# Four subtractions of half blocks placed behind two transform blocks of the last chunk

## The chip, the cores and the metric

The kernel runs on one core of a Trainium2 chip. Its time is the device time of the program in microseconds (us), as the median of several runs. A profile is one execution taken by the hardware profiler; the engines are named as in the profile: PE is TensorE (matmuls; PEld its weight loads), DVE is VectorE, ACT is ScalarE, POOL is GpSimd, SP is SyncE, which here only issues transfers.

## The reference

Two sublayers work on the same normalised input and are added to it. All of it is float32, with S = 2048 tokens, D = 640 and F = 1728.

```python
xn = _layernorm(x, axis=-1)
# A: real part of a Fourier transform over the hidden and then over the sequence dimension
a = einsum("bsd,ed->bse", xn, dft_hid_re)
b = einsum("bsd,ed->bse", xn, dft_hid_im)
A = einsum("ts,bse->bte", dft_seq_re, a) - einsum("ts,bse->bte", dft_seq_im, b)
# B: gated feed-forward
gate = einsum("bsd,df->bsf", xn, W_gate)
up   = einsum("bsd,df->bsf", xn, W_up)
B = einsum("bsf,fd->bsd", (gate * (gate > 0)) * up, W_down)
return x + A + B
```

## The kernel before

The kernel has three stages. The *sequence stage* (up to about 408 us) multiplies the normalised tokens with the two sequence matrices first and leaves the products in DRAM. The *gate stage* makes the gate and up products. The *last stage* multiplies both with the hidden matrices and W_down and adds x.

**Products.** Each float32 product is done as three matmuls: an operand is split into a high part (a rounded copy, ScalarE, L131) and a low part (the operand minus its high part, VectorE, L132), and high x high, high x low and low x high are added in PSUM (`mm3`, L137 to L139). The products are taken over 2 by 2 blocks with seven block products instead of eight, so that sums and differences of blocks are operands: they have the names B11, B12, B21, B22 (blocks) and T1 to T4 (differences).

**The sequence stage** goes through four chunks of 512 output columns (c = 0 to 3). In each chunk the units T1, T2 and B22, T3, T4 follow each other, each over four blocks g = 0 to 3; T2 and B22 alternate (T20 B220 T21 B221 T22 T23 B222 B223). A unit of `stream` loads a block of the transform matrix (L716, tile raw or tk, SP's queue), makes the difference on VectorE (L712), the high part on ScalarE and the low part on VectorE into one of three places of a ring (tile cb), and multiplies it with the resident tokens (xs_early, xs_late) or sums of them (gw). `lows` is the list of the low parts in the order in which they were written, so `lows[-1]` is the latest one.

`drive(4, 2)` writes the steps of the units out: a unit's loads four units ahead of its matmuls, its preparation two ahead. After the preparation of a unit, functions that were registered for it with `at(c, name, g, ...)` are called (`hooks`). `defer(1, f)` calls f one unit later.

**Work for the gate stage** is done beside it with these hooks. `token_sets` normalises transposed tokens in a work area, makes their blocks and differences (L411 to L427), splits them and stores both halves to DRAM (L449, GpSimd's queue). `cross_sets(1, work_pair)` rearranges the fifth part of the hidden dimension: `load` (L464, four loads on GpSimd's queue, 64 partitions each) brings the halves into two places of the work area; `subs` are four subtractions of 128x512 on VectorE (L471): t1 = b12 - b11, t2 = b22 - t1, t3 = b22 - b12, t4 = b21 - t2; `keep` stores seven half blocks to the DRAM tile crossed (L475 and L476, six stores on GpSimd's queue). The load is registered at T1 block 0 of the last chunk.

The work area is the tile `late["work"]` in the pool r1, which has a single buffer. In the last chunk the next tile of r1 takes that buffer: `load_halves` (L789, SP's queue) loads the sets T2, T1 and T3 for the gate stage into it (the units K; a fourth K comes at the end), and other sets into xs_early (the units A). `load_first_cross` (L823, unit X) loads from crossed at the end of the chunk.

**Order.** In the sequence stage no engine's order is written out. A planner decides at build time, engine by engine: among the instructions that are ready by its own estimates, the one that was written first goes first, so that an instruction written much later can be placed early where nothing else is ready. Each engine and each queue then executes in that order, and an instruction that has to wait holds up all that stand behind it. `tc.issue_after(ins)` adds an edge from each instruction written in its block, on the engine of `ins`, to `ins`: it may only be placed behind it, with no wait for its end. `in_turn` uses it to keep a preparation behind the low part of three units earlier. In the gate stage all orders but SP's are written out.

Of the kernel before, what the change touches and what calls it, by code (L numbers as in the profile page):

```python
# [18 lines left out]
NCHUNK = S // CH  # L19
# [16 lines left out]
B11, B12, B21, B22, T1, T2, T3, T4, X4 = range(9)  # L36
# [27 lines left out]
def fnet_reglu_kernel(  # L64
# [17 lines left out]
    keep = ctx.enter_context(tc.tile_pool(name="keep", bufs=1))  # L82
# [59 lines left out]
    lows = []  # L142
# [13 lines left out]
    def defer(units, f):  # L156

        deferred.setdefault(now[0] + units, []).append(f)
# [296 lines left out]
    def cross_sets(q, place):  # L455

        t = {}
        lo, hi = slice(0, HALF), slice(HALF, P)

        def load():  # L460
            t["s"], t["t"] = place(), place()
            for i, r in enumerate((lo, hi)):
                for rows, v in ((lo, 1), (hi, 0)):
                    nc.gpsimd.dma_start(t["s"][rows, i * W2 : (i + 1) * W2], fifth[q][r, v])  # L464

        part = lambda name, i: t[name][:, i * CH : (i + 1) * CH]
        b11, b12, b21, b22 = (lambda i=i: part("s", i) for i in range(4))
        t1, t2, t3, t4 = (lambda i=i: part("t", i) for i in range(4))

        def sub(o, i0, i1):  # L470
            return lambda: nc.vector.tensor_tensor(o().bitcast(F32R), i0(), i1(), op=OP.subtract)  # L471

        def keep():
            for i, part in ((XB11, b11), (XT1, t1), (XT2, t2), (XB21, b21), (XB22, b22)):
                nc.gpsimd.dma_start(crossed[q][:, i * CH : (i + 1) * CH], part())  # L475
            nc.gpsimd.dma_start(crossed[q][:, XT3 * CH : (XT4 + 1) * CH], t["t"][:, 2 * CH : 4 * CH])  # L476

        return load, [sub(t1, b12, b11), sub(t2, b22, t1), sub(t3, b22, b12), sub(t4, b21, t2)], keep
# [357 lines left out]
    def at(c, name, g, *fs):  # L836
        hooks.setdefault((c, name, g), []).extend(fs)
# [12 lines left out]
        at(c, "B22", 2 * i + 1, *([halve["mr"]] if i else halve.values()))  # L850
    load, subs, keep = cross_sets(1, work_pair)
    at(NCHUNK - 1, "T1", 0, load)
    at(NCHUNK - 1, "T2", 3, *subs[:2])
    at(NCHUNK - 1, "B22", 2, *subs[2:], lambda: defer(1, keep))

    def phase(c, names):

# [655 lines left out]
```

## Time and profile before

| | us |
|---|---|
| median of 3 runs | 1030.05 (1028.95 to 1031.12) |
| profiled execution | 1029.97 |
| its span, first to last instruction | 1027.9 |
| TensorE busy | 1014.6 |
| VectorE busy | 808.8 |
| ScalarE busy | 488.1 |
| GpSimd busy | 135.3 |
| longest wait of a matmul | 9.0 |

The chain of work that ended last is 93% TensorE and 4% time without a visible reason. A row of instructions in order of time reads: start, duration, engine, line of the kernel, operation, output tile <- input tiles, shape, count, and in brackets how long the engine was idle ahead of it and what ended that. Matmuls overlap: each is shown with some 0.39 us, though they start about 0.23 us apart.

### The profile page before, as it was taken

The page shows a single profiled execution, that of the slowest core. Times are in us where ns is not written, and L with a number is a line of the kernel's source. Part 1 is how long each engine was busy: PE and PEld are TensorE (multiplying, and loading weights), DVE is VectorE, ACT ScalarE, POOL GpSimd, SP SyncE. Part 2 cuts the span into 40 slices and gives each one's busy share as a digit, 9 for nine tenths or more (in the row PEclk, how much of TensorE's full clock was granted, in tenths as well). Part 3 has the DMA queues.
Part 4 walks back from the last instruction along what each step waited for, and adds up shares of the span by engine and source line. Part 5 has one row for each costly group of instructions (what it writes and reads, how often), then busy time and mean ns, then how long its engine had stood idle before and what let it go on. Part 6 is the DMA issues. An engine that isn't in the chain of part 4 may idle for free.

```text
span 1027.9 us, 12621 instructions
## 1 busy us (share of the span) xinstructions
PE 1014.6 (99%) x4498; PEld 840.0 (82%) x4498; DVE 808.8 (79%) x1085; ACT 488.1 (47%) x659; POOL 135.3 (13%) x215
## 2 busy tenths in 40 slices
PE   9999999999997999999999999999999999999998
PEld 8888888888875888888888888888888888888887
DVE  7957977998967867787777978887586895777983
ACT  5644453443432333555556765555544433543442
POOL 3521001022121001222211000001100000000000
PEclk9999999999998999999999999999999999999999
DMA  8897734968967978657569887784899467896724
GB/s 319 317 306 276 256 125 158 330 225 282 350 207 252 398 292 319 216 195 270 196 217 353 316 281 274 271 300 163 306 400 314 122 233 253 270 331 217 223 92 142
DMA packets 94142, 266.43 MB, mean 259 GB/s; under 512 B 11776, under 2 KB 32832, under 8 KB 91264
## 3 DMA queue, kind: packets, MB, share of 16 engines
q1 hardware_dynamic: 73584, 185.12, 51.8%
q0 software_dynamic: 20064, 79.97, 21.3%
q8 instruction: 35, 0.57, 0.2%
q10 hardware_dynamic: 432, 0.56, 0.2%
q14 instruction: 27, 0.22, 0.1%
HBM read 198.74 MB, written 65.81 MB: 257 GB/s over the span
## 4 chain that ended last, share of the span: by engine, by line
PE 93%; issue 4%; POOL 1%; DVE 1%; DMA 1%; ACT 0%; POOLq 0%; DVEq 0%; ACTq 0%
PE ps L138 27%; PE ps L139 27%; PE ps L137 27%; PE ps L967 4%; PE ps L546 3%; PE ps L970 2%; PE ps L576 1%; PE ps L1358 1%; POOL set L449 1%; DMA cross<-r 0%; PE ps L1363 0%; DVE cb L132 0%; DMA r<-in_x 0%; POOL r L464 0%; POOL pq L685 0%
## 5 line engine op out<-in xcount | busy, mean ns | idle before, releaser
L131 ACT ACTIVATE cb<-rw 128x1024 fp32r<-128x1024 f32 x83 | 81.8, 988 | 136.6 <-PE ps L139 93.3
L131 ACT ACTIVATE cb<-raw 128x1024 fp32r<-128x1024 f32 x71 | 75.2, 1060 | 125.4 <-PE ps L139 117.2
L132 DVE TENSOR_TENSOR cb<-rw,cb 128x1024 fp32r<-128x1024 f32 x83 | 93.9, 1132 | 48.0 <-ACT cb L131 47.7
L132 DVE TENSOR_TENSOR cb<-raw,cb 128x1024 fp32r<-128x1024 f32 x71 | 86.8, 1223 | 37.8 <-ACT cb L131 37.4
L137 PE MATMUL ps<-cb,wt 128*128 128x512 f32 x270 | 105.0, 389 | 0.0
L138 PE MATMUL ps<-cb,wt 128*128 128x512 f32 x270 | 105.0, 389 | 0.0
L139 PE MATMUL ps<-cb,wt 128*128 128x512 f32 x270 | 105.0, 389 | 0.0
L137 PE MATMUL ps<-cb,xs_late 128*128 128x512 f32 x232 | 90.3, 389 | 0.0
L138 PE MATMUL ps<-cb,xs_late 128*128 128x512 f32 x232 | 90.3, 389 | 0.0
L139 PE MATMUL ps<-cb,xs_late 128*128 128x512 f32 x232 | 90.2, 389 | 0.0
L137 PE MATMUL ps<-cb,xs_early 128*128 128x512 f32 x226 | 87.9, 389 | 0.0
L138 PE MATMUL ps<-cb,xs_early 128*128 128x512 f32 x226 | 87.9, 389 | 0.0
L139 PE MATMUL ps<-cb,xs_early 128*128 128x512 f32 x226 | 87.9, 389 | 0.0
L128 ACT ACTIVATE gw<-z 64x512 fp32r<-64x512 f32 (+1 forms) x52 | 46.8, 899 | 49.1 <-PE ps L967 41.7
L937 DVE TENSOR_TENSOR gw<-zs,gw 128x1024 fp32r<-128x1024 f32 x26 | 31.8, 1225 | 42.6 <-ACT gw L128 42.6
L137 PE MATMUL ps<-xs_early,gw 128*128 128x512 f32 x156 | 60.7, 389 | 0.0
L138 PE MATMUL ps<-xs_early,gw 128*128 128x512 f32 x156 | 60.7, 389 | 0.0
L139 PE MATMUL ps<-xs_early,gw 128*128 128x512 f32 x156 | 60.7, 389 | 0.0
L137 PEld LDWEIGHTS ps<-cb,wt 128*128 128x128 f32 x270 | 50.7, 188 | 10.6
L138 PEld LDWEIGHTS ps<-cb,wt 128*128 128x128 f32 x270 | 50.7, 188 | 10.6
L139 PEld LDWEIGHTS ps<-cb,wt 128*128 128x128 f32 x270 | 50.7, 188 | 10.4
L128 ACT ACTIVATE ps<-ps 128x512 f32<-128x512 f32 (+1 forms) x53 | 30.6, 578 | 59.8 <-PE ps L967 55.4
(219 smaller groups left out, 2418.9 us busy)
## 6 DMA issues: line engine op xcount, KB each, us to landing
raw<-in_dft SPq DMA_DIRECT2D x94, 512.0 KB, 6.0
z<-in_wgu SPq DMA_DIRECT2D x26, 896.0 KB, 5.2
wd<-wparts SPq DMA_DIRECT2D x30, 512.0 KB, 5.1
wparts<-pw POOLq DMA_DIRECT2D x12, 1152.0 KB, 4.4
hd<-ob POOLq DMA_DIRECT2D x26, 512.0 KB, 3.8
rw<-hd SPq DMA_DIRECT2D x24, 512.0 KB, 7.3
tk<-in_dft SPq DMA_DIRECT2D x16, 512.0 KB, 7.5
set<-r POOLq DMA_DIRECT2D x16, 512.0 KB, 4.2
```

The lines of the kernel that those rows point to most:

```text
L128: return nc.scalar.activation(o, i, AF.Copy)
L131: nc.scalar.activation(hi, src, AF.Copy)
L132: return nc.vector.tensor_tensor(lo, src, hi.bitcast(F32), op=OP.subtract)
L137: nc.tensor.matmul(ps, wh, mh, start=first, stop=False, skip_group_check=more)
L138: nc.tensor.matmul(ps, wh, ml, start=False, stop=False, skip_group_check=more)
L139: nc.tensor.matmul(ps, wl, mh, start=False, stop=last, skip_group_check=more)
L449: nc.gpsimd.dma_start(place(v), view(part))
L546: start["pe"] = pin([nc.tensor.matmul(E[0, key], xn_part(n * SG + j, d)[v == 1], b[:, int(v == 2), j], start=False, stop=n % NH == NH - 1 ...
L576: pin([nc.tensor.matmul(E[c, key], xn_part(j, d)[v == 1], b[c][0][:, int(v == 2), j], start=j == 0 and v == 0, stop=False)])
L937: tt(self.w[:, o : o + n * 2 * P].rearrange("p (k n) -> p k n", k=n), main(src), main(self.w[:, at : at + n * P3]).bitcast(F32), op=OP.sub ...
L967: nc.tensor.matmul(ps, w[:, a * P3 + 2 * P : (a + 1) * P3], crossing[q, x], start=False, stop=last, skip_group_check=not first)
L970: nc.tensor.matmul(ps, weights[n].w5[:, a : a + P], set_half(q, X4, c)[0], start=False, stop=True, skip_group_check=True)
```

## The change

The two pairs of subtractions are registered at other units of the last chunk, and each pair is written in a block that ties it behind the low part just written. Before, the first pair (t1, t2) was registered at T2 block 3 and the second (t3, t4) at B22 block 2, with no tie; now they are at T2 block 0, behind that block's low part, and at T2 block 1, behind that one's. The stores of `keep` move with the second pair: they are written one unit after the preparation of T2 block 1 instead of one after that of B22 block 2. The load stays where it was. The computation is the same.

```diff
     load, subs, keep = cross_sets(1, work_pair)
     at(NCHUNK - 1, "T1", 0, load)
-    at(NCHUNK - 1, "T2", 3, *subs[:2])
-    at(NCHUNK - 1, "B22", 2, *subs[2:], lambda: defer(1, keep))
+
+    def behind_low(*fs):
+        with tc.issue_after(lows[-1].ins):
+            for f in fs:
+                f()
+
+    at(NCHUNK - 1, "T2", 0, lambda: behind_low(*subs[:2]))
+    at(NCHUNK - 1, "T2", 1, lambda: behind_low(*subs[2:]), lambda: defer(1, keep))
```

## The prediction

> **What bounds the kernel now.** I read the page first, then the busy time by stretches of equal length, then the instructions of one stretch in order of time.
>
> ```profile
> span 1027.9 us, 12621 instructions
> PE 1014.6 (99%) x4498; PEld 840.0 (82%) x4498; DVE 808.8 (79%) x1085; ACT 488.1 (47%) x659; POOL 135.3 (13%) x215
> ```
>
> TensorE sets the time; 13.3 us of the span are not its own. Three stretches of 78 us (columns: length, then busy time and instruction count of each engine, TensorE's clock, DMA share, GB/s), each about one chunk of the sequence stage, show where most of that is:
>
> ```profile
> 178.00:256.00 78.00, 78.00 (x345) 64.57 (x345) 72.14 (x80) 30.57 (x30) 13.86 (x20) 1.00 0.79 273
> 256.00:334.00 78.00, 68.98 (x298) 56.60 (x297) 62.32 (x72) 27.19 (x27) 15.04 (x25) 0.93 0.76 271
> 334.00:412.00 78.00, 78.00 (x346) 64.59 (x345) 58.90 (x63) 28.01 (x30) 5.08 (x10) 1.00 0.86 336
> ```
>
> The stretch before and the one after get 345 and 346 matmuls through, the middle one 298, at a granted clock of 0.93. VectorE in order of time shows why:
>
> ```profile
> 299.07 1.22 DVE L712 TENSOR_TENSOR raw<-tk,raw 128x1024 f32<-128x1024 f32 x1
> 313.63 0.69 DVE L471 TENSOR_TENSOR r<-r 128x512 fp32r<-128x512 f32 x1 [13.34 <-DMA r<-set]
> 314.24 1.22 DVE L132 TENSOR_TENSOR cb<-raw,cb 128x1024 fp32r<-128x1024 f32 x1
> ```
>
> The first of the four L471 subtractions stands in VectorE's queue 13.34 us for its loads. The low part at 314.24, which TensorE needs, stands behind it. TensorE pays:
>
> ```profile
> 306.11 0.39 PE L137 MATMUL ps<-cb,gw 128*128 128x512 f32 x1
> 315.51 0.79 PE L138 MATMUL ps<-cb,gw 128*128 128x512 f32 x1 [9.02 <-DVE cb L132]
> 316.11 0.63 PE L139 MATMUL ps<-cb,gw 128*128 128x512 f32 x1
> ...
> 319.63 0.40 PE L137 MATMUL ps<-cb,xs_late 128*128 128x512 f32 x1
> ```
>
> The loads come late because of GpSimd's queue:
>
> ```profile
> 297.25 0.52 POOL L464 DMA_DIRECT2D r<-set  x1 [1.59 <-DMA set<-r]
> 297.88 0.80 POOL L449 DMA_DIRECT2D set<-r  x1
> 303.13 0.77 POOL L449 DMA_DIRECT2D set<-r  x1 [4.45 <-issue]
> 307.70 0.76 POOL L449 DMA_DIRECT2D set<-r  x1 [3.80 <-issue]
> 308.45 0.55 POOL L464 DMA_DIRECT2D r<-set  x1
> ```
>
> ```profile
> r<-set POOLq DMA_DIRECT2D x1, 256.0 KB, 5.0
> ```
>
> The fourth load stands behind three L449 stores that go out some 5 us apart, issues at 308.45 and lands 5.0 later, at 313.45, which is when the subtraction starts.
>
> **The change, part by part.** All times below are on the clock of this profile; the new one runs earlier behind 306 us by whatever is gained.
>
> 1. *The wait at 300.3 goes.* The subtractions belong to the last chunk, but the planner, which lets ready work of later units fill gaps, had put them into the chunk before. The new edges put the first two behind the low part of T2 block 0 of the last chunk, the others behind that of block 1:
>
> ```profile
> 352.26 1.23 DVE L132 TENSOR_TENSOR cb<-tk,cb 128x1024 fp32r<-128x1024 f32 x1 [1.16 <-ACT cb L131]
> 356.34 1.22 DVE L132 TENSOR_TENSOR cb<-raw,cb 128x1024 fp32r<-128x1024 f32 x1 [2.86 <-ACT cb L131]
> ...
> 360.42 1.23 DVE L132 TENSOR_TENSOR cb<-tk,cb 128x1024 fp32r<-128x1024 f32 x1 [1.72 <-ACT cb L131]
> 361.56 1.22 DVE L712 TENSOR_TENSOR tk<-raw,tk 128x1024 f32<-128x1024 f32 x1
> 363.10 1.23 DVE L132 TENSOR_TENSOR cb<-raw,cb 128x1024 fp32r<-128x1024 f32 x1 [0.31 <-ACT cb L131]
> ```
>
> T2 block 0's low part is at 352.26 and block 1's at 360.42. The loads have been there since 313.45, so nothing waits for them any more. From 306.11 up to 319.63 there start twelve matmuls, those on gw. At the pace of the undisturbed stretch, 78.00 / 345 = 0.226 us, they take 2.71 us; they took 319.63 - 306.11 = 13.52. **TensorE gains 10.8 us**: 9.2 of standing still and 1.6 of the slow pace after it that follows.
>
> 2. *Four subtractions move*, 0.69 each, 2.8 in all. Two land in the gap of 2.86 ahead of 356.34. The other two push the subtraction at 361.56 back by 1.3, and the low part at 363.10 by 1.0 after its own gap of 0.31. Its cover is TensorE's distance:
>
> ```profile
> 368.85 1.06 ACT L131 ACTIVATE cb<-tk 128x1024 fp32r<-128x1024 f32 x1 [1.66 <-PE ps L139]
> ```
>
> Here ScalarE starts on the ring place that TensorE has just left with T2 block 1, and TensorE turns to the block whose low part ends at 364.3: 4.5 us of room. I take 0. Without that cover all 2.8 would count; a gain from their old places there is none, since TensorE ran without gaps around 320 to 334 with them there. Bounds 0 and +2.8.
>
> 3. *The stores of crossed move on GpSimd's queue.* Those of t1, t2 and t3/t4 (the last issued at 330.88, 0.54) now issue at about 354 and 363. The queue is empty there: its store at 346.97 is ahead of them, and the next one stands at 386.37. Cost 0.
>
> 4. *What waits for these stores is late next.* The work area that they read is the only buffer of r1, and the three loads of sets into r1 (L789, SP's queue) need it free:
>
> ```profile
> 330.88 0.54 POOL L476 DMA_DIRECT2D cross<-r  x1 [4.59 <-DVE r L471]
> ...
> 386.37 0.54 POOL L685 DMA_DIRECT2D pq<-sb  x1 [38.86 <-DVE sb L694]
> ```
>
> ```profile
> 341.48 1.28 SPq L789 DMA_DIRECT2D r<-set  x3
> ...
> 364.35 0.33 SPq L716 DMA_DIRECT2D raw<-in_dft  x1
> 368.57 10.07 SPq L789 DMA_DIRECT2D xs_early<-set  x4
> 378.72 6.40 SPq L716 DMA_DIRECT2D raw<-in_dft  x4
> ```
>
> ```profile
> cross<-r POOLq DMA_DIRECT2D x1, 512.0 KB, 7.3
> ```
>
> Today the last store lands at 330.88 + 7.3 = 338.2 and the loads start at 341.48. Afterwards: 361.65 (end of block 1's low part) + 1.3 for two subtractions + 7.3 = **370.3**, 29 us later. Their data is first read in the gate stage, whose first matmul is at 408.04 (quoted below), so that alone costs nothing. But whatever stands behind them in SP's queue waits too, above all the raw blocks of T4, issued from 378.72, and 3 x 1.05 = 3.1 MB move into a time with other transfers:
>
> ```profile
> 340.00:350.00 10.00, 10.00 (x45) 8.26 (x45) 10.00 (x11) 3.19 (x3) 0.53 (x1) 1.00 1.03 424
> 360.00:370.00 10.00, 10.00 (x46) 8.28 (x45) 4.87 (x5) 3.58 (x4) 0.00 (x0) 1.00 0.71 265
> 370.00:380.00 10.00, 10.00 (x46) 8.29 (x45) 7.97 (x8) 3.19 (x3) 0.00 (x0) 1.00 0.65 248
> ```
>
> ```profile
> raw<-in_dft SPq DMA_DIRECT2D x4, 512.0 KB, 7.3
> ```
>
> ```profile
> 388.77 2.35 DVE L712 TENSOR_TENSOR raw<-raw,tk 128x1024 f32<-128x1024 f32 x2
> ```
>
> ```profile
> 397.16 0.39 PE L137 MATMUL ps<-cb,xs_late 128*128 128x512 f32 x1
> ...
> 408.04 0.39 PE L137 MATMUL ps<-xs_early,wr 128*128 128x512 f32 x1
> ```
>
> T4 block 0 lands at 378.72 + 7.3 = 386.0, is subtracted at 388.77 and reaches TensorE at 397.16. Subtraction, high part and low part need 1.22 + 1.06 + 1.23 = 3.5, so data at 393.7 would still do: **7.7 us of room**. From 360 to 380 the transfers leave (424 - 265 + 424 - 248) x 10 us = 3.4 MB free, and 3.1 and 0.5 of the last store want to go there: half a us too much. Even if none of the 3.1 MB found room, it would be 3.1 / 0.424 = 7.3 us, inside the 7.7. I take 0; bounds 0 and, if SP also stands in front of them, about +5.
>
> The Trainium skill ("DMA: Bandwidth & Descriptors", section "Issuing engines are not separate DMA queues") speaks against this move: transfers of all queues end on the same 16 engines and interleave, so that a queue of one's own hides nothing. By that rule the 3.1 MB come out of T4's landing and the sum is the same only because 7.3 is under 7.7; by the rates from 360 to 380 hardly any of it shows. The trace agrees with the rule as far as the full 424 GB/s from 340 to 350, when these loads were running, goes.
>
> Sum: -10.8 + 0 + 0 + 0. The profiled execution took 1029.97, 2.1 more than its span and within 0.1 of the median of the runs, 1030.05. **1030.05 - 10.8 = 1019.2 us.**
>
> **The rivals.** *A, the gain is eaten in part:* part 4's cover is short, T4's blocks arrive 2 to 5 us late, or some other reading of the planner's new order leaves a gap of this size. For it: DMA shares near 1 from 340 to 350. Against: 7.7 us of room. Time: 1021.2 to 1024.2.
>
> *B, slower:* the last store of crossed is placed behind the L685 store at 386.37. Then it lands at 386.91 + 7.3 = 394.2, the three loads start there, and if the four of 368.57 and T4's blocks stand behind them in SP's queue, T4 block 0 lands after 7.8 MB (3.1 + 4.2 + 0.5) at 424 GB/s, 18.4 us later: 412.6, 18.9 behind 393.7. With 1.6 of slow pace TensorE loses 20.5: 1039.7. The point from which it decides: the room is gone when the loads start after 393.7 - 18.4 = 375.3, and the gain is gone when they start after about 386, against 370.3 as worked out. For it: that store has the longest wait in the queue, 38.86. Against it: the subtractions are 20 us ahead of the value that the L685 store waits for.
>
> *C, it doesn't do what it says:* the wait of 13.34 stays, because the next instruction on VectorE needs the same loads, or the low part that is named is one already passed at 300. Neither shows: only L471 reads these loads, and the low part is traced in the last chunk. Time: 1030, no change.
>
> **How the numbers follow.** The forecast 0.78; A 0.12; B 0.05; C 0.05. The forecast's own range is 1018.1 (1.1 lower, as the lowest run, 1028.95, lies under the median) to 1022.0 (+2.8 of part 2). The range takes in A's and half a us for the reading of starts at the low end: **1017.6 to 1024.5**; B and C, 1 in 10, are left out. A measurement tells 0.2% (2.1 us) from no change; forecast and A lie below 1028, C within, B above: faster 0.90, same 0.05, slower 0.05.
>
> **What would show it.** The stretch 256 to 334 with 345 matmuls and a clock of 1.00; no idle time ahead of L471; its first run at about 343 and its third at about 351 on the new clock; L789 into r1 at about 360; no gap of TensorE up to 400. Wrong would be part 1 if VectorE still waits near 300 for anything but ScalarE, part 2 if TensorE waits for L132 near 350, part 4 if it waits near 386 for a low part of T4, with L712 waiting for a raw block ahead of it.

## The result and the profile after

The changed kernel takes 1019.97 us in the median of 5 runs (1019.0 to 1020.7), against 1030.05 before: a ratio of 0.9902, interval 0.9887 to 0.9916. The prediction was 1019.2, with a range of 1017.6 to 1024.5.

The page of the kernel after, first two rows:

```profile
span 1018.1 us, 12626 instructions
PE 1013.0 (99%) x4498; PEld 838.9 (82%) x4498; DVE 810.4 (80%) x1085; ACT 488.3 (48%) x659; POOL 134.8 (13%) x215
```

The same work on every engine, in a span that is 9.8 us shorter. The stretches of 78 us of the kernel after (columns as in the prediction):

```profile
178.00:256.00 78.00, 78.00 (x346) 64.59 (x345) 72.15 (x79) 30.57 (x30) 11.84 (x17) 1.00 0.76 265
256.00:334.00 78.00, 78.00 (x345) 64.57 (x345) 71.88 (x80) 31.45 (x31) 15.88 (x25) 1.00 0.89 325
334.00:412.00 78.00, 78.00 (x346) 64.57 (x345) 57.94 (x66) 28.72 (x35) 8.11 (x15) 1.00 0.85 321
```

The middle one now has 345 matmuls, where it had 298, and a clock of 1.00, where it had 0.93: 47 matmuls of 0.226 us are 10.6 us. VectorE of the kernel after, in order of time, at the old place of the subtractions and at the new one:

```profile
301.54 1.23 DVE L132 TENSOR_TENSOR cb<-raw,cb 128x1024 fp32r<-128x1024 f32 x1 [0.31 <-ACT cb L131]
...
342.38 1.23 DVE L132 TENSOR_TENSOR cb<-tk,cb 128x1024 fp32r<-128x1024 f32 x1 [1.72 <-ACT cb L131]
343.52 1.41 DVE L471 TENSOR_TENSOR r<-r 128x512 fp32r<-128x512 f32 x2
...
350.54 1.22 DVE L132 TENSOR_TENSOR cb<-tk,cb 128x1024 fp32r<-128x1024 f32 x1 [1.72 <-ACT cb L131]
351.69 1.28 DVE L471 TENSOR_TENSOR r<-r 128x512 fp32r<-128x512 f32 x2
```

The low part that stood behind 13.34 us of waiting now starts at 301.54, and the pairs run at 343.52 and 351.69 with no idle time ahead of them. The cause of the late loads is still there. GpSimd's queue of the kernel after:

```profile
298.34 0.80 POOL L449 DMA_DIRECT2D set<-r  x1
303.66 0.77 POOL L449 DMA_DIRECT2D set<-r  x1 [4.53 <-issue]
309.57 0.76 POOL L449 DMA_DIRECT2D set<-r  x1 [5.14 <-issue]
310.32 0.54 POOL L464 DMA_DIRECT2D r<-set  x1
```

The stores still go out 5 to 6 us apart, and the fourth load goes out at 310.32, even later than before. Only VectorE no longer waits for it.

The remaining 0.8 us between 10.6 and 9.8 lie in the opening. Here are the first 100 us, of before and then of after:

```profile
0.00:100.00 100.00, 99.06 (x461) 82.61 (x462) 77.11 (x156) 53.71 (x87) 32.70 (x43) 1.00 0.86 306
```

```profile
0.00:100.00 100.00, 98.25 (x457) 81.68 (x458) 77.92 (x156) 53.39 (x86) 32.48 (x43) 1.00 0.87 303
```

TensorE is busy 0.8 us less there in the one execution of after that was profiled, 200 us ahead of the change. The changed kernel with more room for descriptors (1280 bytes, a run below) is busy 99.21 us of its first 100, and its span is 1017.1, 10.8 under that of before; so the 0.8 us need not come from the change.

### The profile page after: what moved, and what is told of

The parts are those of the page before. It is cut to its first block, busy times and chain, and to the rows that moved or that the text cites. A ratio compares the mean times of both kernels' runs of the same rounds, so it can differ in the third digit from the quotient of the medians.

```text
span 1018.1 us, 12626 instructions
## 1 busy us (share of the span) xinstructions
PE 1013.0 (99%) x4498; PEld 838.9 (82%) x4498; DVE 810.4 (80%) x1085; ACT 488.3 (48%) x659; POOL 134.8 (13%) x215
## 4 chain that ended last, share of the span: by engine, by line
PE 99%; DMA 1%; ACT 0%; ACTq 0%; issue 0%; DVE 0%
PE ps L137 29%; PE ps L138 29%; PE ps L139 29%; PE ps L973 4%; PE ps L546 3%; PE ps L976 2%; PE ps L576 1%; PE ps L1364 1%; DMA raw<-in_lead 1%; PE ps L1369 0%; ACT cb L332 0%; PE ps L1379 0%; ACT y L128 0%; ACTq L613 0%; DVE eps_t L111 0%
## 5 line engine op out<-in xcount | busy, mean ns | idle before, releaser
L132 DVE TENSOR_TENSOR cb<-rw,cb 128x1024 fp32r<-128x1024 f32 x83 | 93.8, 1132 | 48.3 <-ACT cb L131 47.7
L132 DVE TENSOR_TENSOR cb<-raw,cb 128x1024 fp32r<-128x1024 f32 x71 | 86.8, 1223 | 39.9 <-ACT cb L131 39.6
L139 PEld LDWEIGHTS ps<-cb,wt 128*128 128x128 f32 x270 | 50.7, 188 | 10.6
```

Source lines behind the costliest of these rows:

```text
L132: return nc.vector.tensor_tensor(lo, src, hi.bitcast(F32), op=OP.subtract)
L139: nc.tensor.matmul(ps, wl, mh, start=False, stop=last, skip_group_check=more)
```

## The experiments

Every kernel ran beside the kernel before on the same chip; a ratio is to that, with its interval.

### The ties without the move

The subtractions stay registered where they were; only the ties to the two low parts are added.

```diff
-    at(NCHUNK - 1, "T2", 3, *subs[:2])
-    at(NCHUNK - 1, "B22", 2, *subs[2:], lambda: defer(1, keep))
+    for n in range(2):
+        at(NCHUNK - 1, "T2", n, lambda n=n: tied.update({n: lows[-1].ins}))
+    at(NCHUNK - 1, "T2", 3, lambda: behind(0, *subs[:2]))
+    at(NCHUNK - 1, "B22", 2, lambda: behind(1, *subs[2:]), lambda: defer(1, keep))
```

> The two pairs are registered where they were before the change (T2 block 3 and B22 block 2 of the last chunk), and only the ties behind the low parts of T2 blocks 0 and 1 are added. In the order of the program VectorE has them behind those low parts, as in the changed kernel. Theory (the tie does it all): 1020 us, within 1 us of the changed kernel's 1019.97, no matmul waiting for L132. Rival (the earlier registration of the subtractions and of their stores is what gains): 1025 us or more, with the loads into r1 later than 358 us.

Measured: 1020.06 us, ratio 0.9906 (0.9891 to 0.9921). The ties alone give the whole gain; the new places of registration add nothing that can be measured in the time. One matmul waits 0.3 us for L132, where none was expected; part 4 below comes back to it.

### The move without the ties

```diff
-    at(NCHUNK - 1, "T2", 3, *subs[:2])
-    at(NCHUNK - 1, "B22", 2, *subs[2:], lambda: defer(1, keep))
+    at(NCHUNK - 1, "T2", 0, *subs[:2])
+    at(NCHUNK - 1, "T2", 1, *subs[2:], lambda: defer(1, keep))
```

> The two pairs are registered at T2 blocks 0 and 1, without any tie. In the order of the program VectorE has the four subtractions where they stood before the change. Theory: 1030 us, within 1.5 us of the kernel before, with a wait of 12 to 17 us ahead of the first L471 near 300 us and a matmul waiting about 9 us or more for L132. Rival (the registration gains): 1020 us.

Measured: 1030.26 us, ratio 1.0005 (0.9995 to 1.0014). VectorE in order of time, of this kernel:

```profile
313.48 0.69 DVE L471 TENSOR_TENSOR r<-r 128x512 fp32r<-128x512 f32 x1 [12.22 <-DMA r<-set]
```

The planner puts the first subtraction in the same gap near 300, wherever it was registered.

### Only the first pair tied

```diff
-    at(NCHUNK - 1, "T2", 3, *subs[:2])
+    at(NCHUNK - 1, "T2", 0, lambda: behind_low(*subs[:2]))
     at(NCHUNK - 1, "B22", 2, *subs[2:], lambda: defer(1, keep))
```

> Only the first pair is tied behind T2 block 0's low part; the second pair is registered at B22 block 2 without a tie, as before. In the order of the program the third subtraction (t3 = b22 - b12) now stands at the very place that the first one had, behind the second T3 difference of the third chunk; it needs the same fourth load. Theory (the place is what costs, whichever subtraction stands there): no gain, 1030 us, 1028 to 1034, with the 12 to 17 us wait ahead of t3. Rival (the first subtraction's own inputs were the trouble): 1020 us.

Measured: 1029.59 us, ratio 0.9996 (0.9987 to 1.0006). VectorE of this kernel:

```profile
312.60 0.69 DVE L471 TENSOR_TENSOR r<-r 128x512 fp32r<-128x512 f32 x1 [11.88 <-DMA r<-set]
```

Now t3, which needs nothing of the first pair, stands in the gap and waits nearly as long. What costs is the place, not which subtraction stands there; both pairs have to be tied.

### The four loads on another queue

The kernel before, with the four L464 loads of the sequence stage on SP's queue, so that they do not stand behind the stores.

```diff
-                    nc.gpsimd.dma_start(t["s"][rows, i * W2 : (i + 1) * W2], fifth[q][r, v])
+                    (nc.sync if q else nc.gpsimd).dma_start(t["s"][rows, i * W2 : (i + 1) * W2], fifth[q][r, v])
```

> The kernel before, with the four L464 loads of the sequence stage issued from SP's queue instead of GpSimd's, so that they no longer stand behind the three L449 stores. The subtractions float as before; in the order of the program t3 and t1 stand one block earlier, ahead of the low part of B22 block 2. Theory A (what the prediction named: the fourth load behind the stores is what the subtraction waits for): the loads land by about 303 us, the wait shrinks to 3 to 6 us and the time is 1020 to 1023 us. Theory B (the place that t1 is written to must also be free of the last L449 store, issued at 307.70 and landed at 310.8 in the kernel before, and the profile only named the later of two): VectorE still waits until 308 to 312, 10 us or more, and the time stays at 1028 to 1034 us.

Measured: 1031.53 us, ratio 1.0021 (1.0009 to 1.0032). SP's queue, GpSimd's queue and VectorE of this kernel:

```profile
298.61 1.08 SPq L464 DMA_DIRECT2D r<-set  x2
```

```profile
304.85 0.75 POOL L449 DMA_DIRECT2D set<-r  x1 [5.19 <-issue]
308.31 0.76 POOL L449 DMA_DIRECT2D set<-r  x1 [2.70 <-issue]
```

```profile
308.08 0.69 DVE L471 TENSOR_TENSOR r<-r 128x512 fp32r<-128x512 f32 x1 [11.88 <-DMA set<-r]
311.55 0.69 DVE L471 TENSOR_TENSOR r<-r 128x512 fp32r<-128x512 f32 x1 [2.78 <-DMA set<-r]
```

The last loads go out ten microseconds earlier than before, and the wait hardly shrinks: now a store ends it. TensorE waits 11.0 us for a low part, against 9.0, as two of the subtractions now stand ahead of it. The subtractions write into places of the work area that the L449 stores still read, and they start 3.2 us after the stores at 304.85 and 308.31. There were two waits, loads and stores, and the trace of before names the one that came last. Behind both stand the stores that go out some 5 us apart.

### Why the stores go out 5 us apart: more room for descriptors

The idle time ahead of these stores is put down to "issue": no semaphore ends it. A queue without room for the descriptors of the next transfer, the entries that describe it, is one possible reason. The Trainium skill ("DMA: Bandwidth & Descriptors", section "SWDGE vs HWDGE vs iDMA") says that GpSimd itself writes the descriptors of its transfers, into rings kept in SBUF. No row here shows these rings. The kernel sets 1024 bytes per partition aside for descriptors (dynamic_dma_scratch_size). Two sizes were tried, each with the kernel before and the kernel after:

```diff
-    nc = bacc.Bacc("TRN2", target_bir_lowering=False, num_devices=1, dynamic_dma_scratch_size=1024)
+    nc = bacc.Bacc("TRN2", target_bir_lowering=False, num_devices=1, dynamic_dma_scratch_size=4096)
```

> The kernel before with one number changed: 4096 instead of 1024 bytes per partition are set aside for the descriptors of GpSimd's transfers. The order of the program is the same on every engine. Theory (the unexplained 3.8 to 5.3 us ahead of each L449 store are GpSimd waiting for room for descriptors): the stores near 297 to 308 go out about 1 us apart, the fourth load issues before 302 and lands before 307, the wait of the first L471 shrinks from 12-13 us to 3 to 6 us, and the time is 1020 to 1024 us. Rival (GpSimd is held up by VectorE or by the transfers themselves): the stores stay 4 to 5 us apart and the time is 1030 us.

> The changed kernel with 4096 instead of 1024 bytes per partition for the descriptors of GpSimd's transfers. Theory (TensorE is fed without a gap already, so nothing is left for earlier loads to gain): 1020 us, within 1 us of the changed kernel, with the L449 stores about 1 us apart. Rival (other waits of GpSimd still cost something): 1018 us or less.

Measured: before 1027.7 us, ratio 0.9982 (0.9973 to 0.9992); after 1027.79, ratio 0.9983 (0.9973 to 0.9992). In the sequence stage it does what it should. GpSimd's queue and VectorE of the kernel before with 4096:

```profile
292.11 2.31 POOL L449 DMA_DIRECT2D set<-r  x3 [0.97 <-DVE r L132]
294.40 0.54 POOL L464 DMA_DIRECT2D r<-set  x1
```

```profile
301.38 0.69 DVE L471 TENSOR_TENSOR r<-r 128x512 fp32r<-128x512 f32 x1 [0.57 <-DMA r<-set]
```

The three stores go out one behind the other, 0.77 us each, and the wait of the subtraction is 0.57 instead of 13.34. But both kernels lose elsewhere. TensorE's waits from 700 us on, and SP's queue there, with 4096; then SP's queue of the kernel after with 1024:

```profile
PE ps L137 <- ACT wt L131: 5.6, 1, 5.6
```

```profile
716.64 11.66 SPq L1250 DMA_DIRECT2D rw<-pq  x2
```

```profile
717.05 0.81 SPq L1256 DMA_DIRECT2D rw<-pq  x2
```

At the start of the last stage SP's queue stands 11.66 us in one pair of loads, and the weights behind them are late. It waits there for other engines, not for room. Its waits, of the kernel before with 4096:

```profile
SPq L1250 <- DVE gw L132: 7.2, 1, 7.2
SPq L1250 <- PE ps L1363: 3.8, 1, 3.8
```

The second load of the pair goes out only when VectorE has written a tile gw and TensorE has read it; with 1024 and 1280 bytes the same load goes out without these waits. That its tile lies, with 4096, in memory that gw held before is a likely reason, and is not shown. The expectations of these two runs start from one order of the instructions for both sizes. In the last stage the planner, given 4096, orders VectorE and ScalarE differently, but only from some 751 us on, behind these loads. Up to 717 us the kernel before with 4096 is level with the changed one.

So a size was taken at which the planner leaves every engine's order as it was, 1280 bytes:

```diff
-    nc = bacc.Bacc("TRN2", target_bir_lowering=False, num_devices=1, dynamic_dma_scratch_size=1024)
+    nc = bacc.Bacc("TRN2", target_bir_lowering=False, num_devices=1, dynamic_dma_scratch_size=1280)
```

> [...] Theory A (room is counted finely: each store goes out as soon as a quarter more of the earlier ones is done): the stores of L449, 4 to 5 us apart before, come closer, the first L471 starts two or more us before 311.4, and the time is 1020 to 1027 us. Theory B (room is counted in whole transfers, and a quarter more holds no further store): stores, wait ahead of L471 and time stay as before, 1029 to 1031 us.

> The changed kernel with 1280 instead of 1024 bytes per partition for the descriptors; every engine issues in the order of the changed kernel. Both theories: nothing waits for the stores any more, so the time stays at 1019 to 1021 us, with no gap of TensorE behind the opening. A time below 1018 us would show that the changed kernel still pays for the stores somewhere.

Measured: the kernel before 1021.52 us (1021.28 to 1022.47), ratio 0.9922 (0.9905 to 0.9938); the kernel after 1019.46 us (1018.89 to 1020.14), ratio 0.99 (0.9885 to 0.9914). The kernel before with 1280, GpSimd's queue, VectorE, and TensorE's waits:

```profile
291.91 0.80 POOL L449 DMA_DIRECT2D set<-r  x1
295.03 0.77 POOL L449 DMA_DIRECT2D set<-r  x1 [2.32 <-issue]
298.08 0.75 POOL L449 DMA_DIRECT2D set<-r  x1 [2.28 <-issue]
298.82 0.55 POOL L464 DMA_DIRECT2D r<-set  x1
```

```profile
305.22 0.70 DVE L471 TENSOR_TENSOR r<-r 128x512 fp32r<-128x512 f32 x1 [4.78 <-DMA r<-set]
```

```profile
PE ps L138 <- DVE cb L132: 1.5, 2, 1.1
```

Theory A holds. With the same instructions in the same order, a quarter more room brings these stores from 5.2 and 4.6 us apart to 3.1 and 3.0, VectorE's wait from 13.34 to 4.78, TensorE's from 9.0 to 1.5, and 8.8 us off the time. The first L471 starts at 305.22, where it had 313.63. The landings show what GpSimd stands for. With 1024 the store at 297.88 lands 4.9 us after its issue and the next one goes out at 303.13, 0.35 us behind that; this one lands after 4.3, and the next goes out at 307.70, 0.3 behind. With 1280 the stores at 295.03 and 298.08 go out 0.3 to 0.4 us behind the landings of earlier transfers too, but of ones further ahead: the first L464 load (288.76, 6.0 us) and the store two places ahead (291.91, 5.8 us). So with 1024 each of these stores waits until the one ahead of it has landed, and with 1280 more are under way at once. That it is the ring that is full is inferred from this. The changed kernel gains nothing that can be told from it, because nothing that TensorE needs waits for these stores in it. That makes the chain complete: room for descriptors, spacing of the stores, the loads and the places that the stores read, the first subtraction, the low part behind it, TensorE.

### Tied later

The pairs registered where they were, but tied behind the low parts of T2 block 3 and B22 block 2, to see when the work that follows the subtractions becomes late.

```diff
-    at(NCHUNK - 1, "T2", 3, *subs[:2])
-    at(NCHUNK - 1, "B22", 2, *subs[2:], lambda: defer(1, keep))
+    at(NCHUNK - 1, "T2", 3, lambda: behind_low(*subs[:2]))
+    at(NCHUNK - 1, "B22", 2, lambda: behind_low(*subs[2:]), lambda: defer(1, keep))
```

> The two pairs stay registered at T2 block 3 and B22 block 2 and are tied behind the low parts of those units, two and three units later than in the change. In the order of the program the three loads into r1 now stand behind four loads into xs_early and ahead of the fifth and of T4's raw blocks in SP's queue. Prediction's part 4 (room of T4's blocks): the last store of crossed lands near 373 us on the new clock, the loads start there instead of at 358, and T4 block 0 arrives 1 to 2 us after the room is gone: 1020 to 1023 us, with a gap of TensorE of 0 to 3 us near 386 us or L712 waiting for a raw block there. Rival (the room is larger than worked out): 1020 us with no gap at all.

Measured: 1028.38 us, ratio 0.9984 (0.9970 to 0.9998): most of the gain is gone, more than expected. SP's queue, VectorE and TensorE of this kernel:

```profile
374.25 1.27 SPq L789 DMA_DIRECT2D r<-set  x3
...
376.32 2.07 SPq L716 DMA_DIRECT2D raw<-in_dft  x4
```

```profile
390.32 1.23 DVE L712 TENSOR_TENSOR raw<-raw,tk 128x1024 f32<-128x1024 f32 x1 [3.62 <-DMA raw<-in_dft]
```

```profile
392.77 1.22 PE L137 MATMUL ps<-cb,xs_late 128*128 128x512 f32 x2 [6.17 <-ACT cb L131]
```

This is the road of the rivals A and B: the loads into r1 start late, T4's blocks go out behind them, block 0 lands 14.0 us after its issue (376.32 to 390.32), and TensorE stands 6.17 us at it. From 334 to 412 us it gets 307 matmuls through at a mean clock of 0.96, where the kernel after got 346: 39 fewer are 8.8 us.

### Tied in T3

Both pairs registered and tied at T3 blocks 1 and 2.

```diff
-    at(NCHUNK - 1, "T2", 3, *subs[:2])
-    at(NCHUNK - 1, "B22", 2, *subs[2:], lambda: defer(1, keep))
+    at(NCHUNK - 1, "T3", 1, lambda: behind_low(*subs[:2]))
+    at(NCHUNK - 1, "T3", 2, lambda: behind_low(*subs[2:]), lambda: defer(1, keep))
```

> The two pairs are registered at and tied behind T3 blocks 1 and 2, seven units later than in the change. In the order of the program the last store of crossed stands behind the two L685 stores that wait for the B22 results (the place of the prediction's rival B), and in SP's queue T4's raw blocks and two further loads stand ahead of the three loads into r1, the first weights of the gate stage behind them. Prediction's rival B needed T4's blocks behind the loads; here they are not, so T4 costs nothing, the loads start near 386 us on the new clock, and the weights of the gate stage (behind 4.2 MB) come some 8 us later than before: a gap of 0 to 4 us where the gate stage begins, 1020 to 1024 us. Rival (the late release costs the whole gain wherever T4 stands): 1030 us or more.

Measured: 1027.98 us, ratio 0.9983 (0.9972 to 0.9994), again more than expected, and at another place. SP's queue, ScalarE, and TensorE's waits of this kernel:

```profile
368.74 6.40 SPq L716 DMA_DIRECT2D raw<-in_dft  x4
...
386.27 2.12 SPq L789 DMA_DIRECT2D r<-set  x4
...
395.26 15.12 SPq L909 DMA_DIRECT2D z<-in_wgu  x2
```

```profile
405.64 0.63 ACT L128 ACTIVATE gw<-z 64x512 fp32r<-64x512 f32 x1 [12.14 <-DMA z<-in_wgu]
```

```profile
PE ps L137 <- ACT gw L128: 3.2, 1, 3.2
PE ps L137 <- ACT ps L128: 2.6, 1, 2.6
PE ps L139 <- DVE gw L942: 1.1, 1, 1.1
```

Here SP's queue has T4's blocks (368.74) ahead of the loads into r1 (386.27), and T4 is in time. The four loads move 4.2 MB right ahead of the gate stage instead, its first weights (z) are late, ScalarE stands 12.14 us for them, and TensorE waits 6.9 us in all (in the profiled execution, 1031.56 us, the slowest of ten).

## Why the prediction was right, and where not

**Part 1, the wait at 300.3.** Right in size: 47 matmuls more in the stretch are 10.6 us, against 10.8; 0.8 of them are missing from the span in the opening of the profiled execution. Its account of the cause was too short. "The fourth load stands behind three L449 stores" is true of the trace, but putting the loads elsewhere brought nothing; the subtractions wait for the stores as well.

**Rival C** falls: both pairs are in the last chunk. That "the planner had put them into the chunk before" is borne out by the runs that tie only one pair or none.

**Part 2, the four subtractions**, cost 0 as taken. They run at 343.52 and 351.69 where "about 343" and "about 351" stood, and TensorE has no wait behind the opening.

**Part 3, the stores of crossed,** cost 0. GpSimd's queue of the kernel after:

```profile
353.38 0.54 POOL L476 DMA_DIRECT2D cross<-r  x1 [7.49 <-DVE r L471]
376.49 0.55 POOL L685 DMA_DIRECT2D pq<-sb  x1 [22.57 <-DVE sb L694]
```

The last store is 23 us ahead of the L685 store behind which rival B had put it.

**Part 4, what is late next,** is right in the sum, 0, and wrong in its working. The loads into r1 start on time, 358.37 against "about 360". SP's queue of the kernel after, and its T4 loads (number, KB of each, us from issue to landing):

```profile
358.37 1.28 SPq L789 DMA_DIRECT2D r<-set  x3
...
368.85 6.40 SPq L716 DMA_DIRECT2D raw<-in_dft  x4
```

```profile
raw<-in_dft SPq DMA_DIRECT2D x4, 512.0 KB, 13.0
```

T4's loads are issued 9.9 us earlier than the 378.72 of before, like everything behind the wait, but they land in 13.0 us (median; block 0 in 12.0), not in the 7.3 on which the room was worked out. The DMA engines show why:

```profile
360.00:370.00 10.00, 10.00 (x46) 8.28 (x45) 7.91 (x8) 3.22 (x4) 0.00 (x0) 1.00 0.99 417
370.00:380.00 10.00, 10.00 (x45) 8.28 (x45) 6.98 (x8) 2.75 (x3) 1.09 (x2) 1.00 1.00 406
```

From 360 on they are full, at 417 and 406 GB/s. The prediction counted 3.4 MB of free transfer from 360 to 380 and concluded that hardly any of the 3.1 MB would show. But by its own sum the loads start only at 370.3, and what is free ahead of their start is lost: the kernel after moves 233 GB/s from 350 to 360, which is 360 to 370 on the old clock. So 4.7 us of T4 block 0's 7.7 us of room are gone, and by the same account 3.0 are left. The run tied in T3 is the control: there T4's loads go out at 368.74 with the loads into r1 behind them, and block 0 lands in 7.9. What saved the sum was the other bound in that paragraph, 7.3 us if none of the 3.1 MB found room. The rule of the Trainium skill weighed there ("DMA: Bandwidth & Descriptors", section "Issuing engines are not separate DMA queues") spoke for that bound: by it the 3.1 MB come out of T4's landing. The trace agrees with it, with 4.7 us; all these loads are SP's own, so it shows the engines shared, not two queues sharing them.

Part of the 3.0 was luck. The last store landed in 4.9 us and not in the 7.3 reckoned with, and the loads into r1 started 2.0 us ahead of the 370.3 worked out. The run with the ties alone shows how near the edge this is: there the second pair runs up to 2 us later, the loads into r1 start at 359.07 and not at 358.37, T4 block 0 lands in 14.3 us, VectorE stands 1.51 us for it, and the low part of T4's last block is the one for which TensorE waits 0.3 us.

The run tied later fits this smaller room. T4's loads are issued 7.47 us after those of the kernel after (376.32 against 368.85), and block 0 lands in 14.0 instead of 12.0: 9.5 us later, with 3.0 left, makes 6.5; TensorE waited 6.17. Its expectation had been worked out with the 7.7, and that is why it missed. The run tied in T3 missed elsewhere, at the first weights of the gate stage: a gap of 0 to 4 us had been allowed for them. So **rival A's cause was there**, and its condition, "part 4's cover is short", missed by some 3 us. Rival B's **point of decision** was too late as well. It reckoned 18.4 us from the start of the loads into r1 to the landing of T4 block 0; the kernel after took 358.37 to 368.85 + 12.0 = 380.9, that is 22.5. By that the room is gone when the loads start after some 371.2 on the old clock, not 375.3, and with the change they start at 358.37 + 9.9 = 368.3.

## What to carry to other kernels

A wait that the profile puts down to one transfer may be two waits, of which it names the later one; taking away the named one alone shows it. Where GpSimd's stores go out at intervals with "issue" as the cause, look at the room for descriptors before rearranging what waits for them. When a block of loads is moved, take the landing time of the next urgent transfer from a stretch in which the DMA engines are full, not from the quiet stretch of before: the sum here stood on some 3 us where 7.7 were reckoned.

## What was not expected of the hardware

The room for descriptors sets the pace of GpSimd's stores. With 1024, 1280 and 4096 bytes per partition the last two of the three L449 stores start 5.2 and 4.6, 3.1 and 3.0, and 0.77 us after the one ahead of each; with 1024 and 1280 each goes out 0.3 to 0.4 us behind the landing of an earlier transfer. A quarter more was enough for 8.8 of the 10.8 us that the wait cost. For SP's queue these runs show no such effect in the sequence stage: the four T4 loads of the changed kernel take 6.40, 6.39 and 6.40 us to go out with 1024, 1280 and 4096. The changed kernel, with 1280 bytes, is no slower than any other version measured; its 1019.46 us cannot be told from the 1019.97 of the change alone.
